# A top-k attention and two MLPs on one core: the products of p and v issued in one run, batch norms summed before their product

## The chip, the cores and the metric

The kernel runs on one core of a Trainium2 chip. The metric is the device time of one execution in microseconds (us): the median of the runs shown. All engines of the core work from queues of their own, each in the order in which its instructions were put there: PE (TensorE, matrix products; its weight loads are listed apart as PEld), DVE (VectorE), ACT (ScalarE), POOL (GpSimd) and SP (SyncE, which here issues DMAs).

## What is computed

The inputs q, k and v have the shape 4 x 8 x 576 x 64 (batch, heads, rows, columns), and the weights of each MLP are 512 x 2048 and 2048 x 512. The weights arrive as 64-bit floats, which the kernel converts itself.

```python
scores = scale * np.matmul(q, k.transpose(0, 1, 3, 2))
kth = np.partition(scores, -top_k, axis=-1)[..., -top_k:-top_k + 1]   # top_k = 32
scores = np.where(scores >= kth, scores, -1000000000.0)
scores = scores - np.max(scores, axis=-1, keepdims=True)
attn = np.exp(scores)
attn = attn / (np.sum(attn, axis=-1, keepdims=True) + 1e-09)
x = np.matmul(attn, v)                    # then to (B * S, H * D) = 2304 x 512
h = x @ w_in;  g = np.maximum(h, 0.0) + np.log1p(np.exp(-np.abs(h)));  x = g @ w_out
h = x @ w_in2; g = h - np.tanh(h);                                     out = g @ w_out2
```

## The kernel before

**Numbers.** Each operand of a product is split into a high and a low half of 16 bits, scaled by a power of two, and each product is the sum of three: high by high, high by low, low by high. The power of two comes from a sum of squares over the whole operand. `norm` (L332) takes it for one tensor of one batch: five pieces of 128 x 460 are loaded (L341), ACT squares each and leaves its row sums in one column of a tile `vss` of 128 x 5 (L343), and `col_norm` (L164) adds up partitions and columns on PE, by five products of one column with a matrix of ones (L169), accumulated in a tile `pn`. `pow2_scale` turns the sum into the scale and its inverse by three small DVE operations (L176, L179, L180). `v_norm` and `qk_norm` call it, for v and for q and k of a batch; the main loop does so at the tiles listed in `v_norm_at` and `qk_norm_at` (tiles 0, 4, 12 and 16, and for batches 2 and 3 tiles 40, 44, 56 and 60). Weight blocks, first visits and the MLP's middle activation go through `col_norm` too, with their own columns (`ss`, `qss`, `yss`).

**Attention.** It is cut into 144 tiles. 128 are normal: 128 rows of one head. Each head has 64 rows left over, and 16 further *left* tiles hold those of two heads. A tile goes through `front` (PE makes the scores `s`, L554; ACT copies them to `ssb`, L557), `chain` (DVE finds the 32 largest by four MAX8 and three MATCH_REPLACE8, L566 and L569), `exps` and `mask` (ACT, DVE L590), `turn` (ACT and POOL split p into halves `hl`, L596 to L598; SP issues a transposing DMA from `hl` to `pT`, L600) and `back`: PE multiplies `pT` by `vhl` into `px` (L612 to L617), ACT adds a small number to the sum column (L628), DVE takes its reciprocal (L629), ACT scales (L636). The product of a normal tile is 14 matmuls of 65 columns with weights of 128 x 128. That of a left tile is 28: 14 for each of two heads, with weights of 128 rows by 64 columns, which the profile shows as `128*64`.

**MLPs.** Their steps are fed in between, about one step of 256 rows for each attention tile: `gemm1` (24 products `h`, L680 to L682), `act1`, and some steps later `gemm2` (24 or 12 products `y`, L723 to L733). Weight conversion fills the first 420 us.

**Order.** The code is recorded in the order of the main loop; a scheduler then decides, engine by engine, in which order instructions are issued. It goes by a modelled timeline and by priorities: code under `tc.high_priority(n)` counts as if it stood n instructions earlier. `back` is called under `HP` = 50, as are `front` and `chain`; the first steps of the weight conversion have 100 and `act1` 100. On PE the order is fixed once made: an instruction that waits holds up all behind it.

Of the kernel before, what the change touches and what calls it, by code (L numbers as in the profile page):

```python
# [8 lines left out]
F32 = mybir.dt.float32  # L9
# [5 lines left out]
ALU = mybir.AluOpType  # L15
AX = mybir.AxisListType
# [51 lines left out]
LSP = 2  # L68
HID = 0
HP = 50  # L70


@with_exitstack
def topk_attention_two_mlps(
# [17 lines left out]
    nc = tc.nc  # L92
    P = 128
    B, H, S, D = q.shape
# [3 lines left out]
    NB = 4  # L98
# [46 lines left out]
    def tiny(n=1):  # L145
        o = used_[0]
        used_[0] += n
        return tiles_[:, o : o + n]
# [24 lines left out]
    def pow2_scale(ps, s, inv):  # L173

        n = sp.tile([P, 1], I32, tag="n0", name=nm("n0"))
        nc.vector.tensor_scalar(n, ps.bitcast(I32), 24, 23,  # L176
                                op0=ALU.logical_shift_right, op1=ALU.logical_shift_left)

        nc.vector.tensor_scalar(s.bitcast(I32), n, -1.0, float(204 << 23), op0=ALU.mult, op1=ALU.add)  # L179
        nc.vector.tensor_scalar(inv.bitcast(I32), n, float(50 << 23), None, op0=ALU.add)  # L180
# [150 lines left out]
    def norm(x, b, s, inv):  # L331
        xf = x[b].rearrange("h s d -> (h s d)").rearrange("(p n) -> p n", p=P)  # L332
        n = H * S * D // P
        np_ = -(-n // 512)
        w = n // np_ // 2 * 2
        ss = sp.tile([P, np_], F32, tag="vss", name=nm("vss"))
        for i in range(np_):
            o, e = i * w, (i + 1) * w if i < np_ - 1 else n
            j, st = xy_take([P, 512], F32, "vst")
            st = st[:, : e - o]  # L340
            nc.sync.dma_start(st, xf[:, o:e])  # L341
            xy_free.append(j)
            nc.scalar.activation(st, st, AF.Square, accum_out=ss[:, i : i + 1])  # L343
        pow2_scale(col_norm(ss, np_), s, inv)

    def v_norm(b):

        norm(v, b, sx[b], ix[b])

    def exp_scale(iq, ik, es, nes, nst):  # L350
        nc.vector.scalar_tensor_tensor(es, iq, QK, ik, op0=ALU.mult, op1=ALU.mult)
# [1 line left out]
        nc.vector.tensor_scalar(nst, es, -STEP, None, op0=ALU.mult)  # L353

    def qk_norm(b):
        norm(q, b, sq[b], iq[b])
        norm(k, b, sk[b], ik[b])
        exp_scale(iq[b], ik[b], es[b], nes[b], nst[b])

    def visit_norm(vi):  # L360

# [240 lines left out]
    def back(st):  # L602
        vi, it = st.vi, st.it
        ps = ps_t.tile([P, 512], F32, tag="tp", name=nm("px"))
        if st.kind == "n":
            sides = [(ps[:, 0 : D + 1], st.h, 0, P)]
        else:
            sides = [(ps[0:SL, j * (D + 1) : (j + 1) * (D + 1)], j, j * SL, (j + 1) * SL) for j in range(2)]
        for o, h, c0, c1 in sides:
            vh, vl = vi.vhl[:, 0, h], vi.vhl[:, 1, h]  # L610
            for t in range(NB):
                nc.tensor.matmul(o, st.pT[:, t, c0:c1], vh[:, t, 0 : D + 1], start=(t == 0), stop=False)  # L612
                nc.tensor.matmul(o, st.pT[:, t, c0:c1], vl[:, t, 0 : D + 1], start=False, stop=False)
                nc.tensor.matmul(o, st.pT[:, NB + 1 + t, c0:c1], vh[:, t, 0 : D + 1], start=False, stop=False)
            nc.tensor.matmul(o, st.pT[:, NB, c0:c1], vh[:, NB, 0 : D + 1], start=False, stop=False)

            nc.tensor.matmul(o, st.pT[:, NB, c0:c1], vl[:, NB, 0 : D + 1], start=False, stop=True)  # L617
        if st is it.sts[0]:
            it.x = ap.tile([P, 2, P], F16, tag="xs", bufs=NXS, name=nm("xs"))
            if XE:  # L620
                it.x32 = ap.tile([P, P], F32, tag="x32", bufs=NXS, name=nm("x32"))
        rows = P if st.kind == "n" else SL
        ns = len(sides)
        r = sp.tile([P, 2], F32, tag="r2", bufs=3, name=nm("r2"))

        pv = ps[0:rows, 0 : ns * (D + 1)].rearrange("p (j d) -> p j d", j=ns)
        rr = r[0:rows, 0:ns].unsqueeze(2)
        nc.scalar.activation(rr, pv[:, :, D : D + 1], AF.Identity, bias=(eps2 if st.soft else eps)[0:rows])  # L628
        nc.vector.reciprocal(r[0:rows, 0:ns], r[0:rows, 0:ns])  # L629
# [12 lines left out]
        if XE:  # L642
            if XE == 1:
                nc.scalar.copy(it.x[0:rows, 0, :], it.x32[0:rows])
            else:
                nc.vector.tensor_copy(it.x[0:rows, 0, :], it.x32[0:rows])
            nc.gpsimd.tensor_sub(it.x[0:rows, 1, :], it.x32[0:rows], it.x[0:rows, 0, :])
        nc.sync.dma_start_transpose(
            out=it.chunk.x.block(vi.p)[:, :, it.col : it.col + rows],
            in_=it.x[0:rows].rearrange("p r c -> p (r c)"),  # L650
        )
# [293 lines left out]
    c1 = [0]  # L945
# [55 lines left out]
        nonlocal_credit[0] -= st[0].T / 256.0  # L1001

    nonlocal_credit = [0.0]

    ensure_load(1)
    for i in range(LA - 1):
# [4 lines left out]
    for n in range(-1, NT + 2 + BL):  # L1011
        cur, prv, old, last = [tiles[i] if 0 <= i < NT else None for i in (n, n - 1, n - 2, n - 2 - BL)]
        if cur is not None:
          with tc.high_priority(HP):
            chain(cur)
            cur.ops[0]()
        if prv is not None:
          with tc.high_priority(HP):
            prv.ops[4]()
        if old is not None:  # L1020
            with tc.high_priority(HP):
                mask(old)
                turn(old)
        if last is not None:
            ch = last.it.chunk
            if not hasattr(ch, "x"):
                while ch.T // P > len(xy_free):
                    force_step(n - 2 - BL)
                ch.x = new_xy(ch.T, "x")
            with tc.high_priority(HP):  # L1030
                back(last)
        if n + 1 < NT and n + 1 >= 0:
            st = tiles[n + 1]
            st.vi = st.spec["vi"]
            with tc.high_priority(HP):
                front(st)
        if 0 <= n + LA < NT:
          with tc.high_priority(HP):
            prep_for(tiles[n + LA])
        if 0 <= n + 8 < NT:  # L1040
            ensure_load(tiles[n + 8].spec["i"] + 1)
        if n == VN:
            v_norm(0)
        if cur is not None and n >= VN and not hasattr(cur.vi, "vdone"):
            with tc.high_priority(HP):
                visit_prep_v(cur.vi)
                cur.vi.vdone = True
        if n >= 0:
            emit_steps(n - 2 - BL, 1)
            if n in qk_norm_at:  # L1050
                qk_norm(qk_norm_at[n])
            if n in v_norm_at and n > 0:
                b = v_norm_at[n]
                v_norm(b)
                if b % 2:
                    nc.vector.tensor_tensor(sxl[b // 2], sx[b - 1], sx[b], op=ALU.min)
                    nc.vector.tensor_tensor(ixl[b // 2], ix[b - 1], ix[b], op=ALU.max)
                    for c in (b - 1, b):
                        nc.vector.tensor_mul(fl[c], sxl[b // 2], ix[c])
            wcred[0] += WPS if wi[0] < 16 else (WPS2 if n >= W2N else 0)  # L1060
            while wcred[0] >= 1:
                wcred[0] -= 1
                conv_step()
            load_more()
        for i in (1, 2, 3):
          with tc.high_priority(HP):
            if cur is not None:
                cur.ops[i]()
            if prv is not None and i < 3:
                prv.ops[4 + i]()  # L1070
        if prv is not None:
            with tc.high_priority(HP):
                exps(prv)
# [34 lines left out]
```

## Time and profile before

| | |
|---|---|
| median of 3 runs | 1321.21 us (1319.98 to 1322.13) |
| the profiled execution | 1321.81 us |
| its span, first to last instruction | 1320.0 us |
| PE busy | 1040.3 us, 79% |
| DVE busy | 1015.6 us, 77% |
| ACT busy | 959.3 us, 73% |
| POOL busy | 843.6 us, 64% |

Busy time counts an instruction from its start to its end; products on PE overlap, so the time from one start to the next says more of them than their duration. The granted clock is the share of 2.4 GHz that TensorE got: 1.00 is 2.4 GHz and 0.50 is 1.2 GHz; a value between is a mean over both. In the chain of work that ended last, PE holds 47% of the span, DVE 16%, DMA 10%, POOL and ACT 9% each.

### The profile page before, as it was taken

The numbers are of one execution on the slowest core, as the hardware profiler recorded it, in microseconds if no ns is written. First come the engines' busy times: TensorE is split into PE (matmuls) and PEld (weight loads), VectorE is DVE, ScalarE is ACT, GpSimd is POOL, SyncE is SP. The second block draws the span as 40 slices with busy tenths as digits, with TensorE's granted clock in tenths as the row PEclk, the third lists the DMA queues.
The fourth block names the chain that finished last, engine by engine and source line by source line (L and its number), as shares of the span: only waits on it lengthen the run. The fifth ranks groups of instructions, "written<-read, shape, count | busy, mean of one in ns | idle before, by whom it ended". The sixth has DMA issues, their size and how long they took to land.

```text
span 1320.0 us, 27592 instructions
## 1 busy us (share of the span) xinstructions
PE 1040.3 (79%) x9778; PEld 811.4 (61%) x9778; DVE 1015.6 (77%) x2171; ACT 959.3 (73%) x1924; POOL 843.6 (64%) x1194
## 2 busy tenths in 40 slices
PE   2230335793347999899898999998999899999998
PEld 1120224682336876667666897676767777986975
DVE  5996988999999798977789889967889899610020
ACT  7987997987877788775778777758767777643332
POOL 2689865896877576565577766747776467643332
PEclk9999995896558999988899999989999899999999
DMA  8955886456565756644556444544445344300000
GB/s 270 289 173 154 251 215 150 116 122 159 128 146 133 173 102 151 139 87 85 108 114 130 94 87 89 104 95 95 110 97 116 71 93 96 51 6 9 9 9 16
DMA packets 322522, 153.14 MB, mean 116 GB/s; under 512 B 270160, under 2 KB 302416, under 8 KB 322384
## 3 DMA queue, kind: packets, MB, share of 16 engines
q1 hardware_dynamic: 322384, 151.39, 49.5%
q8 instruction: 76, 1.25, 0.4%
q14 instruction: 62, 0.51, 0.1%
HBM read 73.04 MB, written 15.37 MB: 67 GB/s over the span
## 4 chain that ended last, share of the span: by engine, by line
PE 47%; DVE 16%; DMA 10%; POOL 9%; ACT 9%; issue 8%; SPq 1%; POOLq 0%; ACTq 0%; DVEq 0%
PE h L682 7%; PE h L680 7%; PE h L681 7%; DVE m L566 5%; DVE x L569 5%; PE y L731 4%; PE y L732 4%; PE y L733 4%; PE y L723 3%; PE y L724 3%; PE y L725 3%; PE s L554 3%; POOL wlo L316 2%; DMA pT<-hl 2%; DVE x L590 2%
## 5 line engine op out<-in xcount | busy, mean ns | idle before, releaser
L566 DVE MAX8 m<-x 128x8 f32<-128x576 f32 x432 | 319.2, 749 | 3.4
L702 POOL TENSOR_SCALAR r<-r,gs 128x512 f32<-128x512 f32 (+1 forms) x160 | 109.3, 684 | 172.3 <-ACT g L701 168.7
L597 POOL TENSOR_TENSOR hl<-x,hl 128x512 f16<-128x512 f32 x144 | 172.7, 1199 | 71.5 <-ACT hl L596 58.6
L569 DVE MATCH_REPLACE8 x<-m,x 128x576 f32<-128x576 f32 x288 | 213.1, 740 | 0.0
L554 PE MATMUL s<-kT,qT 128*128 128x288 f16 x512 | 116.8, 321 | 97.9 <-ACT ssb L557 71.8
L705 POOL TENSOR_TENSOR g<-r,g 128x512 f16<-128x512 f32 (+1 forms) x160 | 172.8, 1080 | 8.8
L680 PE MATMUL h<-y,whi 128*128 128x256 f16 (+1 forms) x640 | 164.5, 265 | 5.9 <-ACT y L751 5.2
L681 PE MATMUL h<-x,whi 128*128 128x256 f16 (+1 forms) x640 | 166.7, 268 | 0.0
L680 PE MATMUL h<-x,whi 128*128 128x256 f16 (+1 forms) x640 | 166.5, 268 | 0.2
L682 PE MATMUL h<-x,wlo 128*128 128x256 f16 (+1 forms) x640 | 166.5, 268 | 0.0
L723 PE MATMUL y<-g,whi 128*128 128x256 f16 (+1 forms) x640 | 163.8, 266 | 2.8 <-DVE mx L420 2.7
L724 PE MATMUL y<-g,whi 128*128 128x256 f16 (+1 forms) x640 | 164.0, 265 | 1.4 <-POOL g L705 1.4
L681 PE MATMUL h<-y,whi 128*128 128x256 f16 (+1 forms) x640 | 164.2, 265 | 0.0
L725 PE MATMUL y<-g,wlo 128*128 128x256 f16 (+1 forms) x640 | 164.1, 266 | 0.0
L682 PE MATMUL h<-y,wlo 128*128 128x256 f16 (+1 forms) x640 | 164.0, 265 | 0.0
L699 DVE SCALAR_TENSOR_TENSOR r<-h,hin,r 128x512 f32<-128x512 f32 (+1 forms) x80 | 55.1, 690 | 141.1 <-ACT r L134 140.3
L134 ACT ACTIVATE r<-h,hin 128x512 f32<-128x512 f32 (+1 forms) x160 | 102.2, 640 | 82.7 <-PE h L682 69.4
L612 PE MATMUL px<-vhl,pT 128*128 128x65 f16 (+1 forms) x640 | 98.0, 208 | 67.9 <-DMA pT<-hl 55.1
L701 ACT ACTIVATE g<-r,gs 128x512 f16<-128x512 f32 (+1 forms) x160 | 107.8, 676 | 54.4 <-PE y L724 21.1
L566 DVE MAX8 m<-ssb 128x8 f32<-128x576 f32 x144 | 107.9, 750 | 42.5 <-ACT ssb L557 42.0
L680 PEld LDWEIGHTS <-whi 128*128 128x128 f16 x1280 | 127.5, 100 | 19.7
L681 PEld LDWEIGHTS <-whi 128*128 128x128 f16 x1280 | 127.1, 99 | 19.8 <-issue 1.8
(140 smaller groups left out, 3178.7 us busy)
## 6 DMA issues: line engine op xcount, KB each, us to landing
whi<-in_moe_w_in_dram SPq DMA_DIRECT2D x8, 1024.0 KB, 5.7
wlo<-in_moe_w_in_dram SPq DMA_DIRECT2D x6, 1024.0 KB, 7.2
wlo<-in_moe_w_out_dram SPq DMA_DIRECT2D x6, 1024.0 KB, 5.2
vd<-vhl SPq DMA_DIRECT2D x16, 330.0 KB, 2.9
vhl<-vd SPq DMA_DIRECT2D x16, 330.0 KB, 3.2
kd<-kT SPq DMA_DIRECT2D x32, 160.0 KB, 2.2
whi<-in_moe_w_out_dram SPq DMA_DIRECT2D x5, 1024.0 KB, 5.0
kT<-kd SPq DMA_DIRECT2D x32, 160.0 KB, 2.6
```

The lines of the kernel that those rows point to most:

```text
L554: nc.tensor.matmul(ps[:, hf, 0:HS], lhs, rhs[:, hf * HS : (hf + 1) * HS], start=(i == 0), stop=(i == len(prods) - 1))
L566: return lambda: nc.vector.max(m[:, 8 * i : 8 * i + 8], src)
L569: return lambda: nc.vector.match_replace(x, m[:, 8 * i : 8 * i + 8], src, NEG)
L597: nc.gpsimd.tensor_sub(hl[:, S + SL : 2 * S], st.p[:, 0 : NB * P], hl[:, 0 : NB * P])
L680: nc.tensor.matmul(o, hi[:, f], xhi, start=(d == 0), stop=False)
L681: nc.tensor.matmul(o, hi[:, f], xlo, start=False, stop=False)
L682: nc.tensor.matmul(o, lo[:, f], xhi, start=False, stop=(d == ND - 1))
L702: nc.gpsimd.tensor_scalar(r, r, gs, 1.0, op0=ALU.mult, op1=ALU.mult)
L705: nc.gpsimd.tensor_sub(glo, r, ghi)
L723: nc.tensor.matmul(o, hi[:, dd], gh, start=first, stop=False)
L724: nc.tensor.matmul(o, hi[:, dd], gl, start=False, stop=False)
L725: nc.tensor.matmul(o, lo[:, dd], gh, start=False, stop=fin)
```

## The change

`back` issues its products under a priority of 1000 instead of 50. `norm` returns a function that ends it: the five columns of `vss` are first summed on DVE to one column, which then goes through a single product in `col_norm`. For norms met at tile 20 or later that end is recorded two tiles after the squares. `vss` has two buffers by name.

```diff
+HPB = 1000
@@ norm
-        pow2_scale(col_norm(ss, np_), s, inv)
+        def finish():
+            tot = tiny()
+            nc.vector.tensor_reduce(tot, ss, axis=AX.X, op=ALU.add)
+            pow2_scale(col_norm(tot, 1), s, inv)
+        return finish
@@ back
-        for o, h, c0, c1 in sides:
-            ...
+        with tc.high_priority(HPB):
+            for o, h, c0, c1 in sides:
+                ...
@@ main loop
             if n in qk_norm_at:
-                qk_norm(qk_norm_at[n])
+                ends_at.setdefault(n if n < 20 else n + 2, []).append(qk_norm(qk_norm_at[n]))
...
+            for e in ends_at.pop(n, ()):
+                e()
```

What the scheduler makes of it. On PE, at left tile 64 (counted from 0; `px_7022` is its product, `pT_6909` its weights, `h` and `y` products of an MLP). Before, from the middle of the tile:

```order
L725 MATMUL y_6866<-g_6550,wlo_92 128x256
L613 LDWEIGHTS pT_6909
L613 MATMUL px_7022<-vhl_6505,pT_6909 64x65
L682 LDWEIGHTS wlo_90
L682 MATMUL h_6946<-x_3737,wlo_90 128x256
L614 LDWEIGHTS pT_6909
L614 MATMUL px_7022<-vhl_6505,pT_6909 64x65
L680 LDWEIGHTS whi_89
```

The same product now (`px_6986`; lines are 11 further down):

```order
L691 MATMUL h_6910<-x_3719,whi_89 128x256
L623 LDWEIGHTS pT_6873
L623 MATMUL px_6986<-vhl_6452,pT_6873 64x65
L624 LDWEIGHTS pT_6873
L624 MATMUL px_6986<-vhl_6452,pT_6873 64x65
L625 LDWEIGHTS pT_6873
L625 MATMUL px_6986<-vhl_6452,pT_6873 64x65
L623 LDWEIGHTS pT_6873
```

The 28 products stood in 27 pieces with MLP products between them, and stand in one. Over the kernel the 448 products of left tiles stood in 118 pieces and stand in 16; the 1792 of normal tiles stood in 543 pieces and stand in 198. The 70 joints that stay open there are between two normal tiles that alternate.

On PE, at normal tile 49, what stands ahead of its product. Before (`px_5362`):

```order
L733 MATMUL y_5138<-whi_95,g_4986 128x512
L731 LDWEIGHTS g_4985
L731 MATMUL y_5137<-whi_95,g_4985 128x512
L612 LDWEIGHTS pT_5261
L612 MATMUL px_5362<-vhl_4952,pT_5261 128x65
```

Now (`px_5335`):

```order
L692 LDWEIGHTS whi_93
L692 MATMUL h_5271<-y_3983,whi_93 128x256
L693 LDWEIGHTS wlo_94
L693 MATMUL h_5271<-y_3983,wlo_94 128x256
L623 LDWEIGHTS pT_5234
L623 MATMUL px_5335<-vhl_4925,pT_5234 128x65
```

It has moved ahead of 31 `y` products of 512 columns that stood before it.

## Rows read from the trace of the kernel before

**Rows 1.** The page: busy share in tenths over 40 equal slices, granted clock.

```profile
PE   2230335793347999899898999998999899999998
DVE  5996988999999798977789889967889899610020
PEclk9999995896558999988899999989999899999999
```

**Rows 2.** Busy time by stretch: start:end, length, engines (instructions), PE clock, DMA.

```profile
core 0: us, PE busy (x) PEld busy (x) DVE busy (x) ACT busy (x) POOL busy (x), PEclk, DMA share, GB/s
0.00:420.00 420.00, 180.97 (x1490) 143.06 (x1491) 373.34 (x808) 355.52 (x718) 307.04 (x392) 0.83 0.68 179
556.00:1010.00 454.00, 431.54 (x4180) 330.22 (x4181) 381.74 (x794) 330.04 (x664) 300.24 (x464) 0.96 0.48 100
1160.00:1320.00 160.00, 155.37 (x1360) 117.94 (x1356) 19.09 (x36) 53.79 (x86) 56.63 (x73) 1.00 0.03 10
```

**Rows 3.** Timeline of PE, left tile 64: start, duration, both us; full clock.

```profile
599.04 0.28 PE L680 MATMUL h<-x,whi 128*128 128x256 f16 x1
599.25 0.22 PE L615 MATMUL px<-vhl,pT 128*64 128x65 f16 x1
599.40 0.28 PE L681 MATMUL h<-x,whi 128*128 128x256 f16 x1
599.61 0.22 PE L617 MATMUL px<-vhl,pT 128*64 128x65 f16 x1
```

**Rows 4.** Timeline of PE, normal tile 81, full clock.

```profile
727.60 0.27 PE L682 MATMUL h<-x,wlo 128*128 128x256 f16 x1
727.71 0.19 PE L614 MATMUL px<-vhl,pT 128*128 128x65 f16 x1
727.74 0.27 PE L680 MATMUL h<-x,whi 128*128 128x256 f16 x1
```

**Rows 5.** Timeline of PE, left tile 64 and after it, half clock.

```profile
603.35 0.39 PE L682 MATMUL h<-x,wlo 128*128 128x256 f16 x1
603.67 0.26 PE L612 MATMUL px<-vhl,pT 128*64 128x65 f16 x1
603.87 0.39 PE L680 MATMUL h<-x,whi 128*128 128x256 f16 x1
...
606.35 0.42 PE L723 MATMUL y<-g,whi 128*128 128x256 f16 x1
606.56 0.42 PE L724 MATMUL y<-g,whi 128*128 128x256 f16 x1
```

**Rows 6.** Busy time by stretch, around left tile 64; columns as in rows 2.

```profile
593.00:602.00 9.00, 9.00 (x60) 5.52 (x57) 8.75 (x19) 5.14 (x10) 5.43 (x9) 1.00 0.27 67
602.00:606.00 4.00, 4.00 (x18) 1.82 (x18) 0.06 (x1) 0.66 (x1) 0.00 (x0) 0.53 0.00 0
606.00:609.00 3.00, 3.00 (x16) 2.13 (x16) 2.62 (x6) 1.74 (x6) 0.61 (x2) 0.50 0.52 98
```

**Rows 7.** Timeline of PE, unbroken normal tile 77 and left tile 90, first and last.

```profile
703.69 0.20 PE L612 MATMUL px<-vhl,pT 128*128 128x65 f16 x1 [1.21 <-DMA pT<-hl]
...
704.10 0.19 PE L617 MATMUL px<-vhl,pT 128*128 128x65 f16 x1
...
794.28 0.22 PE L612 MATMUL px<-vhl,pT 128*64 128x65 f16 x1
...
795.16 0.19 PE L617 MATMUL px<-vhl,pT 128*64 128x65 f16 x1
795.28 0.28 PE L680 MATMUL h<-y,whi 128*128 128x256 f16 x1
```

**Rows 8.** Waits from 300 us on: us in total, times, longest.

```profile
PE px L612 <- DMA pT<-hl: 16.6, 11, 4.1
DVE r L629 <- ACT r L628: 29.1, 10, 8.7
PE pn L169 <- ACT vst L343: 6.3, 5, 1.9
```

**Rows 9.** Tiles pn (400 to 560 us) and pT, line L416: ns min/median/max.

```profile
L169 PE MATMUL pn<-vss,tiny x60: 164/250/270, 408.3 to 556.3; 128*128 128x1 f32 x60
L416 DVE TENSOR_REDUCE mx<-t x6: 140/146/149, 150.7 to 536.6; 128x1 f32<-128x8 f32 x6
L612 PEld LDWEIGHTS <-pT x640: 95/98/292, 62.1 to 1160.3; 128*128 128x128 f16 x128, 128*64 128x64 f16 x32
DMA to landing us min/median/max: 3.2/3.3/7.4
```

**Rows 10.** Timeline of SP and PE, normal tile 49.

```profile
483.81 1.24 SPq L600 DMA_TRANSPOSE pT<-hl  x1
...
488.96 0.38 PE L731 MATMUL y<-whi,g 128*128 128x512 f16 x1
489.17 0.19 PE L612 MATMUL px<-vhl,pT 128*128 128x65 f16 x1
```

More of the change, by code (lines that the diff above doesn't have):

```diff
@@ L335, in norm @@
         w = n // np_ // 2 * 2
-        ss = sp.tile([P, np_], F32, tag="vss", name=nm("vss"))
+        ss = sp.tile([P, np_], F32, tag="vss", bufs=2, name=nm("vss"))
         for i in range(np_):
@@ L343, in norm @@
             nc.scalar.activation(st, st, AF.Square, accum_out=ss[:, i : i + 1])
-        pow2_scale(col_norm(ss, np_), s, inv)
+        def finish():
[3 more added lines that the diff above has]
+        return finish
     def v_norm(b):
-        norm(v, b, sx[b], ix[b])
+        return norm(v, b, sx[b], ix[b])
     def exp_scale(iq, ik, es, nes, nst):
@@ L355, in qk_norm, with finish @@
     def qk_norm(b):
-        norm(q, b, sq[b], iq[b])
-        norm(k, b, sk[b], ik[b])
-        exp_scale(iq[b], ik[b], es[b], nes[b], nst[b])
+        ends = norm(q, b, sq[b], iq[b]), norm(k, b, sk[b], ik[b])
+        def finish():
+            for e in ends:
+                e()
+            exp_scale(iq[b], ik[b], es[b], nes[b], nst[b])
+        return finish
     def visit_norm(vi):
@@ L608, in back @@
             sides = [(ps[0:SL, j * (D + 1) : (j + 1) * (D + 1)], j, j * SL, (j + 1) * SL) for j in range(2)]
-        for o, h, c0, c1 in sides:
[L610 to L617, printed above, removed]
+        with tc.high_priority(HPB):
+            for o, h, c0, c1 in sides:
+                vh, vl = vi.vhl[:, 0, h], vi.vhl[:, 1, h]
+                for t in range(NB):
+                    nc.tensor.matmul(o, st.pT[:, t, c0:c1], vh[:, t, 0 : D + 1], start=(t == 0), stop=False)
+                    nc.tensor.matmul(o, st.pT[:, t, c0:c1], vl[:, t, 0 : D + 1], start=False, stop=False)
+                    nc.tensor.matmul(o, st.pT[:, NB + 1 + t, c0:c1], vh[:, t, 0 : D + 1], start=False, stop=False)
+                nc.tensor.matmul(o, st.pT[:, NB, c0:c1], vh[:, NB, 0 : D + 1], start=False, stop=False)
+                nc.tensor.matmul(o, st.pT[:, NB, c0:c1], vl[:, NB, 0 : D + 1], start=False, stop=True)
         if st is it.sts[0]:
@@ L1003, in topk_attention_two_mlps, with left_scales @@
     nonlocal_credit = [0.0]
+    ends_at = {}
+    def left_scales(b):
+        nc.vector.tensor_tensor(sxl[b // 2], sx[b - 1], sx[b], op=ALU.min)
+        nc.vector.tensor_tensor(ixl[b // 2], ix[b - 1], ix[b], op=ALU.max)
+        for c in (b - 1, b):
+            nc.vector.tensor_mul(fl[c], sxl[b // 2], ix[c])
     ensure_load(1)
@@ L1042, in topk_attention_two_mlps @@
         if n == VN:
-            v_norm(0)
+            v_norm(0)()
         if cur is not None and n >= VN and not hasattr(cur.vi, "vdone"):
@@ L1050, in topk_attention_two_mlps @@
             if n in qk_norm_at:
-                qk_norm(qk_norm_at[n])
+                ends_at.setdefault(n if n < 20 else n + 2, []).append(qk_norm(qk_norm_at[n]))
             if n in v_norm_at and n > 0:
                 b = v_norm_at[n]
-                v_norm(b)
+                ends_at.setdefault(n if n < 20 else n + 2, []).append(v_norm(b))
                 if b % 2:
[L1056 to L1059, printed above, removed]
+                    ends_at[n if n < 20 else n + 2].append(lambda b=b: left_scales(b))
+            for e in ends_at.pop(n, ()):
+                e()
             wcred[0] += WPS if wi[0] < 16 else (WPS2 if n >= W2N else 0)
```

## The prediction

> **What bounds the kernel now.** I read the slices first, then the stretches, then PE's timeline inside the stretch that PE bounds. In the slices [rows 1] DVE leads up to about 420 us and PE from there on; after 1160 us only PE has work. The stretches say it in numbers [rows 2]. Up to 420 us DVE is busy for 373 us, PE for 181. From 556 to 1010 us PE is busy for 431.5 of 454 us and DVE for 381.7: PE stands still for 22 us, every other engine for over 70. After 1160 us it is PE alone, with 155 of 160. So from 556 us on time taken off PE is time taken off the end, as long as the others keep up.
>
> Busy is not useful, though. In that stretch PE has places where it is busy all the time and gets little done. In left tile 64, 602 to 606 us, PE is busy for 4.00 of 4.00 us and issues 18 products, while DVE is busy for 0.06, ACT for 0.66 and POOL not at all [rows 6]: the whole core waits for PE. The timeline shows why [rows 3]. A product of 64 weight columns (`128*64`) alternates there with an MLP product of the full array, and from one MLP product to the next it takes 0.36 us (599.04 to 599.40). Where the product of a normal tile is woven in in the same way, full array both, it takes 0.14 us (727.60 to 727.74) [rows 4]. So weaving as such is free (an MLP product takes 0.11 of it and px 0.03), but each change between 64 columns and 128, there and back, costs 0.22 us more. At the half clock a round takes 0.52 us (603.35 to 603.87) [rows 5].
>
> **The change part by part.** *Left tiles in one run.* The order has 118 pieces of left-tile products before and 16 after, so 102 rounds go. In the trace of before all but one of the 102 lie between 557 and 1009 us, in seven tiles, 77 at the full clock and 25 at half of it. At the full clock: 77 x (0.36 - 0.14) = 16.9 us. At the half clock a woven full-array round would take 0.21 (606.35 to 606.56) [rows 5] and twice 0.03, some 0.27: 25 x (0.52 - 0.27) = 6.3 us if the clock falls there all the same, and 25 x (0.52 - 0.14) = 9.5 us if it doesn't. The 28 products that are left in a run take 0.88 us and one change at either end, as left tile 90 does already (794.28 to 795.16) [rows 7]. I take 26.4 us, with 23.2 as the lower end. All of it is on PE in the stretch that PE bounds.
>
> *The clock.* It is 1.00 from 593 to 602 us, 0.53 from 602 to 606 and still 0.50 from 606 to 609, when ordinary MLP products run again [rows 6]. It fell while PE, by its busy time, never paused, in the middle of the alternation; the same happens in tiles 59 and 100, and together the three leave 11 us of ordinary work at half speed, worth up to 5.5 us. If the alternation brings it down, that comes back. If something else does, nothing. I take 4, the nearer row being that two of the three falls come late in the longest alternations.
>
> The Trainium skill, on the page "TensorE: Matmul & The Clock Gate" (Part 1: The HAM clock gate), ties the half rate to an idle engine. Rows 6 show a fall without a pause, so by that rule read plainly this part would be 0 and the sum 4 us less.
>
> *Normal tiles in one run.* 1792 products in 543 pieces become 198. A piece costs nothing by rows 4, so I take 0. Within a tile the last product comes some 1.3 us sooner (1.7 us from first to last where a tile is woven in, 0.41 in tile 77 [rows 7]), and DVE's reciprocal, which waited for 29.1 us in ten places from 300 us on [rows 8], waits less; that is part of how the other engines get their share of the gain, not a gain of its own.
>
> *The batch norms.* Six norms lie between 400 and 560 us, with 60 instructions on PE (two for each product) of 250 ns [rows 9]. 48 of them go, 24 products, 6 to 12 us depending on how far the two of a product overlap, and the waits of PE for the squares, 6.3 us [rows 8], go with them since the end is asked for two tiles later. Much of that lies where weight conversion and DMA still set the pace: bounds 0 and 18, I take 5. The 12 sums on DVE cost about what the reduction of 128 x 8 at L416 does, 0.146 us [rows 9]: 12 x 0.146 = 1.8 us, half of it where DVE leads. I take 1 us as a loss. What is queued behind them on DVE is the chain of the tile at hand; the squares they need lie two tiles back, so they should not wait.
>
> *What the higher priority moves.* The products of p and v stand earlier on PE, and PE holds everything behind one that waits for its `pT`. Before, 11 of some 120 tiles from 300 us on waited, 16.6 us in all [rows 8]; the others found their tile landed. Most tiles keep their place to within 1 us of matmul time. Seven stand 3 to 7.5 us earlier (42, 45, 49, 54, 58, 88, 89). Tile 49 is an example: its transpose is issued at 483.81, lands some 3.3 us later at the soonest [rows 9], and the product starts at 489.17 behind `y` products of 0.21 us each [rows 10], 31 of which it now passes, 6.6 us. Adding up for the seven what they move beyond what their tile had been waiting in memory gives some 15 us, and 18 with crumbs elsewhere: bounds 0 and 18. I take 5, since a wait of PE there lets DVE and ACT catch up and PE's later waits shrink.
>
> *The first 420 us.* Nearly every engine's order is shuffled there by a few places. DVE's idle time, 420 - 373 = 47 us [rows 2], is a bound on any gain; no row prices a loss. I take 0, with 6 to either side as in a few per cent of that idle time and a few weight passes.
>
> *What the others can't follow.* PE stands idle for 5% of 556 to 1010 us; with 30 us less work and DVE at 382 of 424, I let that grow to 10% of what is freed: 3 us lost.
>
> Sum: 26.4 + 4 + 5 - 1 - 5 - 3 = 26.4 us. The profiled execution took 1321.81, so 1295.4; the median of the runs stands 0.6 lower: 1295.
>
> **The rivals.** *The gain is half swallowed.* DVE, ACT and the transposes take PE's place in the stretch. From 640 us on slices with DVE at nine tenths are common [rows 1], and a tile needs about 5.5 us of DVE against some 6 of PE. Against it: in the broken tiles the other engines stand still [rows 6], so they gain their time there too. If half of the 30 us is lost: 1307.
>
> *PE waits for `pT`, and it ends slower.* The place is the head of PE's queue, L612 from 420 to 1160 us. The seven tiles give 18 us; and if the 16.6 us of waits that are there double, since less work stands ahead of each product, that is 35 us against 35 gained before this term and the last (26.4 + 4 + 5). It decides from about 35 us of new waits; with the norms' 5 us not coming either, 1321.8 - 30 + 35 = 1327. For it: on this queue the products now go before work that was ready. Against it: 110 of 120 tiles had landed, most for 1 to 8 us.
>
> *A run of small products is bound by its weight loads.* A load for these products lasts 98 ns [rows 9]; woven in, it lies under the MLP product ahead, 0.11 us long. If in a run each product took its load's 98 ns instead of 30, the 345 closed joints of normal tiles would cost 345 x 0.07 = 24 us, and the sum would come to 1321.8 - 26.4 + 24 = 1319. Against it: tile 77 runs its 14 in 0.41 us already, 30 ns each [rows 7]. The loads overlap each other.
>
> The Trainium skill states a load's time by its columns ("TensorE: Matmul & The Clock Gate", LDWEIGHTS), an estimate of 107 ns for 128 columns. By that rule the run would be load-bound, as this rival has it, and the kernel would come out at about 1322. The page also has a faster load for full 16-bit weights (Weight-path perf modes), and rows 7 side with that.
>
> *The change does not do what it says.* The order shows that it does on PE; only the time could fail to follow, which is the first rival.
>
> **How the numbers follow.** Forecast, 14 to 39 us gained: 0.76. Half swallowed, 3 to 14 gained: 0.13. PE's waits, slower: 0.05. Load-bound runs: 0.02, of which half ends within 0.2%. The rest, a first stage gone wrong or a mixture that ends near 1321: 0.04. A change of 0.2%, 2.6 us, is about what a measurement of this kernel can tell. Faster by more: 0.89; within: 0.05; slower: 0.06. The range takes in, above, 23.2 from the rounds, nothing from the clock, 2 from the norms, waits of 10 and the losses of 1 and 3 (11 us gained, 1311) and, below, 26.4 from the rounds, 5.5 from the clock, 10 from the norms, 1 lost to the sums and no waits (41 us gained, 1281).
>
> **What would show it.** In the profile after, left tiles appear as one run of 28 in about 0.9 us, and no stretch like 602 to 606 us is left, with DVE, ACT and POOL at rest. The stretch from tile 59 to tile 120, 556 to 1008 us before, takes 25 to 30 us less, and the time after the last attention tile stays at about 160 us. The clock is 1.00 around tiles 59, 64 and 100. `pn` from `vss` is gone and 12 reductions are there. I am wrong if PE's waits for `pT` grow by more than 15 us, if DVE is at 95% of the stretch, or if the first 420 us get longer.

## The result, and the profile after

The changed kernel took 1303.78 us, the median of 4 runs (1299.76 to 1307.39), against 1320.60 us for the kernel before beside it (1312.04 to 1322.13). The ratio is 0.9881, with a 95% interval from 0.9853 to 0.9910: 16.8 us gained, where 26 were forecast. The time lies inside the predicted range. The profiled execution of the changed kernel took 1306.19 us, 15.6 less than that of before.

The first view is the page of the kernel after, its slices, to be laid beside [rows 1].

```profile
PE   1221324884436999899799899998999899999998
DVE  5897889999999998899698879988989799510020
PEclk9999999896557999999799989998999899999999
```

DVE still leads up to about 420 us and PE behind it. From there to the last attention tile DVE is now mostly at eight or nine tenths, and the clock's slow places in the PE stretch stand elsewhere than before. The second view is the busy time by stretch, with the stretches of [rows 2] (the last ends with the span): start:end, length, each engine's busy time with its instructions, granted clock, DMA share, GB/s.

```profile
0.00:420.00 420.00, 172.40 (x1450) 133.94 (x1451) 370.29 (x812) 354.50 (x716) 308.00 (x393) 0.87 0.70 179
556.00:1010.00 454.00, 425.15 (x4329) 339.32 (x4328) 400.70 (x827) 344.34 (x690) 311.90 (x480) 0.97 0.50 104
1160.00:1304.00 144.00, 139.40 (x1137) 102.76 (x1134) 17.07 (x33) 47.33 (x75) 51.22 (x66) 1.00 0.03 10
```

By busy time the first 420 us are what they were. In the middle stretch PE gets through 149 more products in the same 454 us (4329 against 4180), and DVE is busy for 400.7 us instead of 381.7. So work was freed on PE and the others followed; but PE's own idle time has grown, from 22 to 29 us. The third view is PE's timeline at left tile 64 (start, duration, both in us), which answers to [rows 3].

```profile
588.05 0.27 PE L691 MATMUL h<-x,whi 128*128 128x256 f16 x1
588.25 0.22 PE L623 MATMUL px<-vhl,pT 128*64 128x65 f16 x1
...
589.13 0.19 PE L628 MATMUL px<-vhl,pT 128*64 128x65 f16 x1
589.34 0.27 PE L734 MATMUL y<-g,whi 128*128 128x256 f16 x1
```

The 28 products now take 0.88 us from the first to the last, with one change of columns at either end; before, they were strewn over some 12 us (593.9 to 605.8). The fourth view gives the waits from 300 us on (us in total, times, longest), beside [rows 8].

```profile
PE s L564 <- ACT ssb L567: 41.0, 21, 4.7
PE pn L170 <- ACT wlo L289: 30.1, 7, 10.0
DVE r L640 <- ACT r L639: 26.0, 16, 8.7
PE px L623 <- DMA pT<-hl: 10.0, 12, 2.0
```

The kernel before has for the first of these:

```profile
PE s L554 <- ACT ssb L557: 41.6, 17, 9.1
```

PE's waits for `pT` did not grow with the higher priority; they fell from 16.6 to 10.0 us, and the longest from 4.1 to 2.0. The waits for the copy of the scores are the same in sum, 41.0 and 41.6 us, but lie elsewhere, as is shown below. Those for `wlo`, 30.1 us, all lie ahead of 404 us, where DVE leads.

**Where the time came from.** A fixed amount of PE work can be compared in the two traces. I took PE's products in their order, without those of norms, each with its columns (at least 64) at 2.4 GHz, and looked at the part from 208 to 590 us of such work: 551.7 to 1013.6 us in the kernel before, 551.8 to 995.4 in the kernel after. The work is 382.2 us in both; it is an equal amount of work, not product for product the same, since the orders differ. What lies above it was put down to the reason at each product: a half clock, a change between 64 and 128 weight columns, PE idle ahead of the next product (wait), a norm's product, other.

| us | before | after | difference |
|---|---|---|---|
| length of the part | 461.9 | 443.6 | -18.3 |
| changes of columns | 27.9 | 3.5 | -24.4 |
| waits | 24.6 | 29.3 | +4.7 |
| half clock | 12.1 | 11.9 | -0.2 |
| products of norms | 4.0 | 4.6 | +0.6 |
| other | 11.1 | 12.2 | +1.1 |

Ahead of that part the kernel after is 0.1 us behind, and behind it it loses 2.3 us. Together that is 15.9 us gained; the profiled executions differ by 15.6.

**The new waits.** The waits of PE from 556 to 1010 us, the kernel before and then the kernel after:

```profile
PE px L612 <- DMA pT<-hl: 8.1, 6, 2.1
PE s L554 <- ACT ssb L557: 4.8, 4, 2.2
```

```profile
PE s L564 <- ACT ssb L567: 14.1, 10, 4.4
PE px L623 <- DMA pT<-hl: 5.3, 6, 2.0
```

What is late now is the copy of the scores: PE may write the next scores only when ACT has copied older ones, and it waits there for 14.1 us instead of 4.8. The longest such wait shows the clock as well. Busy time by stretch around it, and PE's line at its end:

```profile
735.00:745.00 10.00, 9.93 (x114) 8.99 (x113) 6.15 (x13) 7.53 (x16) 6.02 (x9) 1.00 0.33 67
745.00:750.00 5.00, 0.67 (x6) 0.52 (x6) 2.75 (x4) 3.45 (x7) 3.69 (x7) 0.99 0.00 0
750.00:757.00 7.00, 6.40 (x62) 5.78 (x61) 6.79 (x18) 4.63 (x13) 4.09 (x10) 0.52 0.40 84
```

```profile
749.33 1.08 PE L564 MATMUL s<-kT,qlT 128*128 128x288 f16 x6 [4.40 <-ACT ssb L567]
```

PE runs through ten busy microseconds, stands for 4.4, and has half the clock for the 7 that follow. A little earlier ACT and then DVE had been held up, which the same timeline shows on their engines:

```profile
735.89 0.62 ACT L513 CAST qhl<-qraw 128x512 f16<-128x512 f32 x1 [4.31 <-DMA qT<-qhl]
```

```profile
738.82 0.17 DVE L640 RECIPROCAL r<-r 128x1 f32<-128x1 f32 x1 [2.79 <-ACT r L639]
```

ACT waited 4.3 us for a buffer whose transpose was still under way, DVE then 2.8 us for ACT. That these led to PE's wait 10 us later is a reading of the order of events; no run tested it.

### The profile page after: what moved, and what is told of

Same layout as the page of the kernel before. It is cut to its first block, busy times and chain, and to the rows that moved or that the text cites. A ratio compares the mean times of both kernels' runs of the same rounds, so it can differ in the third digit from the quotient of the medians.

```text
span 1304.4 us, 27426 instructions
## 1 busy us (share of the span) xinstructions
PE 1007.8 (77%) x9682; PEld 793.1 (61%) x9682; DVE 1020.7 (78%) x2183; ACT 959.4 (74%) x1924; POOL 844.0 (65%) x1194
## 4 chain that ended last, share of the span: by engine, by line
PE 29%; DVE 22%; ACT 13%; DMA 13%; POOL 12%; issue 8%; SPq 2%; POOLq 0%; ACTq 0%; DVEq 0%
DVE m L576 7%; DVE x L579 7%; PE h L692 4%; PE h L691 4%; PE h L693 4%; DMA pT<-hl 2%; POOL hl L607 2%; PE y L735 2%; DMA qT<-qhl 2%; PE y L736 2%; PE y L734 2%; PE y L742 2%; PE y L743 2%; PE y L744 2%; POOL wlo L317 2%
## 5 line engine op out<-in xcount | busy, mean ns | idle before, releaser
L713 POOL TENSOR_SCALAR r<-r,gs 128x512 f32<-128x512 f32 (+1 forms) x160 | 112.5, 704 | 160.9 <-ACT g L712 158.8
L564 PE MATMUL s<-kT,qT 128*128 128x288 f16 x512 | 120.2, 326 | 98.2 <-ACT ssb L567 69.9
L734 PE MATMUL y<-g,whi 128*128 128x256 f16 (+1 forms) x640 | 163.1, 266 | 10.5 <-DVE y L763 6.9
L692 PEld LDWEIGHTS <-whi 128*128 128x128 f16 x1280 | 128.3, 100 | 23.4 <-issue 7.6
L693 PEld LDWEIGHTS <-wlo 128*128 128x128 f16 x1280 | 128.6, 101 | 13.7
L135 ACT ACTIVATE x<-ssb,nb,tiny 128x576 f32<-128x576 f32 x144 | 123.7, 865 | 15.3 <-DVE m L576 10.8
```

Source lines behind the costliest of these rows:

```text
L135: table[1].append(nc.scalar.activation(out, in_, func, **kw))
L564: nc.tensor.matmul(ps[:, hf, 0:HS], lhs, rhs[:, hf * HS : (hf + 1) * HS], start=(i == 0), stop=(i == len(prods) - 1))
L692: nc.tensor.matmul(o, hi[:, f], xlo, start=False, stop=False)
L693: nc.tensor.matmul(o, lo[:, f], xhi, start=False, stop=(d == ND - 1))
L734: nc.tensor.matmul(o, hi[:, dd], gh, start=first, stop=False)
```

## The experiments

Thirteen kernels in all, the changed one and twelve others, each compared with the kernel before on the same chip. The expectations number their theories, and each says what its theories are. Two numbers stand for the two halves of the kernel in the profiled execution of each: when the first 170 us of PE work (as above) were done, and how long the part from 208 to 590 us of work took. "Priority" is the high priority of the products of p and v.

| kernel | priority for | norms | median us | ratio, 95% | 170 us done at | part | changes | waits | half clock |
|---|---|---|---|---|---|---|---|---|---|
| before | none | old | 1320.6 | | 507.7 | 461.9 | 27.9 | 24.6 | 12.1 |
| after | all | new | 1303.8 | 0.9881 (0.9853 to 0.9910) | 508.8 | 443.6 | 3.5 | 29.3 | 11.9 |
| px_only | all | old | 1316.1 | 0.9987 (0.9966 to 1.0008) | 525.4 | 442.5 | 5.0 | 34.4 | 3.7 |
| norm_only | none | new | 1326.0 | 1.0065 (1.0036 to 1.0093) | 507.1 | 459.0 | 30.1 | 17.9 | 13.5 |
| full_before | none | old | 1313.6 | 0.9956 (0.9932 to 0.9980) | 510.2 | 444.7 | 0 | 37.1 | 9.2 |
| normal_only | normal tiles | old | 1336.1 | 1.0133 (1.0111 to 1.0155) | 519.6 | 468.6 | 28.3 | 23.4 | 16.0 |
| late_px | tiles from 48 | old | 1303.4 | 0.9861 (0.9837 to 0.9885) | 506.9 | 444.2 | 4.5 | 31.6 | 8.8 |
| late_left | left tiles from 48 | old | 1301.1 | 0.9845 (0.9816 to 0.9874) | 506.2 | 444.8 | 2.8 | 33.7 | 8.8 |
| late_after | tiles from 48 | new | 1299.9 | 0.9834 (0.9811 to 0.9858) | 512.3 | 442.3 | 2.9 | 31.4 | 9.3 |
| full_after | all | new | 1306.5 | 0.9879 (0.9851 to 0.9908) | 509.7 | 444.4 | 0 | 32.1 | 13.1 |
| early_px | tiles to 47 | old | 1344.9 | 1.0176 (1.0137 to 1.0215) | 523.2 | 472.9 | 28.1 | 27.2 | 19.8 |
| early_after | tiles to 47 | new | 1326.6 | 1.0054 (1.0024 to 1.0084) | 505.6 | 466.0 | 30.7 | 17.8 | 21.4 |
| nodelay | all | sum only | 1306.6 | 0.9888 (0.9846 to 0.9931) | 514.0 | 441.9 | 3.3 | 33.1 | 8.4 |
| delay5 | all | delay only | 1313.4 | 0.9943 (0.9920 to 0.9966) | 516.6 | 449.5 | 4.3 | 37.6 | 8.3 |

The kernel before took 1318.1 us (median) beside px_only to normal_only, 1320.7 beside late_px to full_after and 1320.5 beside the last four. One profiled execution stands beside each median, and runs of one kernel differ by some 5 us to either side, so single entries of the last five columns are read with that in mind, and the pattern rather than any one of them.

### The two halves apart: px_only and norm_only

The priority alone, with the norms as before:

```diff
+HPB = 1000
...
-        for o, h, c0, c1 in sides:
+        with tc.high_priority(HPB):
+            for o, h, c0, c1 in sides:
                 ...
```

> The kernel before with the first half of the change alone: the products of p and v under the priority of 1000, the norms as before. Left-tile products stand in 16 pieces, normal ones in 198, as with the whole change. If the gain is the joints of 64-column products (theory 1), this takes all of it: 1300 to 1308 us. If the sum of the norm's columns brings some 5 us of it (theory 3), it ends at 1306 to 1313.

And the norms alone, the priority left at 50 (of the norm's edit, two lines):

```diff
+            nc.vector.tensor_reduce(tot, ss, axis=AX.X, op=ALU.add)
+            pow2_scale(col_norm(tot, 1), s, inv)
```

> The second half alone: one product for a batch norm, two tiles late, and the products of p and v under the priority of before. The scheduler then lays the left-tile products in 174 pieces, 56 more than before. Theory 1: 56 rounds at 0.22 us are 12 us of PE, of which three quarters or so reach the end: 1325 to 1335, slower than before. Theory 3, the norm's own gain: 1313 to 1318.

px_only missed: with all the left tiles whole it gained nothing that can be told from 0. norm_only came out slower, as expected: by 0.4 to 0.9%. The reason expected for it, 56 more rounds, is not shown: most of them lie ahead of 545 us, the changes of columns in the part cost 30.1 us against 27.9, and the profiled execution, 1323.3 us, is only 1.5 longer than that of the kernel before. So neither half is faster by itself, and both together are, by 17 us; the parts don't add up. The table says where px_only lost it: its part from 208 us on is as short as that of the kernel after, but the first 170 us of work were done 17.7 us late. Most of the loss lies between 318 and 432 us. Busy time by stretch there, of px_only, and below of the kernel before and the kernel after:

```profile
318.00:432.00 114.00, 50.41 (x409) 38.39 (x406) 104.35 (x236) 84.38 (x207) 78.37 (x127) 0.57 0.55 124
```

```profile
318.00:432.00 114.00, 60.44 (x536) 48.41 (x534) 111.50 (x255) 89.89 (x223) 86.57 (x137) 0.65 0.59 137
```

```profile
318.00:432.00 114.00, 59.33 (x492) 46.90 (x493) 108.92 (x252) 91.76 (x228) 84.60 (x134) 0.60 0.61 143
```

DVE sets the pace here: 111.5 of 114 us in the kernel before. In px_only it is busy for 104.4 and has done 19 instructions fewer. The waits of PE in the same stretch, two lines of the kernel before and then those of px_only:

```profile
PE s L554 <- ACT ssb L557: 21.4, 7, 8.0
PE px L612 <- DMA pT<-hl: 7.7, 3, 4.1
```

```profile
PE s L555 <- ACT ssb L558: 36.1, 10, 7.2
PE px L614 <- DMA pT<-hl: 10.1, 3, 5.5
PE pn L170 <- ACT vst L344: 4.5, 1, 4.5
```

And one wait of DVE in px_only:

```profile
DVE m L567 <- ACT ssb L558: 4.5, 3, 2.4
```

PE's waits for the copy of the scores have grown by 14.7 us, those for `pT` by only 2.4, the longest from 4.1 to 5.5. DVE, which in the kernel before never waited for scores in this stretch, does so for 4.5 us. That a wait for `pT` at the head of PE's queue, with products of scores behind it, is what starts this is a reading of these lines; no run isolates it.

### Left tiles without a change of columns: full_before

The kernel before, but the products of a left tile use all 128 weight columns. The left rows of the second head of each left tile are left out by this. The number of products is the same; their order is not quite: products of left tiles stand in 123 pieces and those of normal tiles in 590 (118 and 543 before), and PE's order leaves that of the kernel before at 250 us.

```diff
-            sides = [(ps[0:SL, j * (D + 1) : (j + 1) * (D + 1)], j, j * SL, (j + 1) * SL) for j in range(2)]
+            sides = [(ps[:, j * (D + 1) : (j + 1) * (D + 1)], j, 0, P) for j in range(2)]
...
-            sc, src = r[0:rows, i : i + 1], o[:, 0:D]
+            sc, src = r[0:rows, i : i + 1], o[0:rows, 0:D]
```

> The kernel before, with the products of left tiles made on the full array: weights of 128 columns for each of the two heads, with the rows of both in the result and the first 64 kept (the second head's 64 left rows are so left out). Their products still stand between MLP products, in 123 pieces; normal ones in 590. Theory 1 (a change of weight columns is what costs): 20 us less PE, 1298 to 1308. Theory 2 (what costs is that the product is torn, whatever its columns): 1318 to 1326, as before.

The timeline of PE in left tile 64, still in pieces:

```profile
594.35 0.27 PE L682 MATMUL h<-x,wlo 128*128 128x256 f16 x1
594.46 0.19 PE L612 MATMUL px<-vhl,pT 128*128 128x65 f16 x1
594.49 0.27 PE L680 MATMUL h<-x,whi 128*128 128x256 f16 x1
594.60 0.19 PE L613 MATMUL px<-vhl,pT 128*128 128x65 f16 x1
```

And busy time by stretch there, the clock at 1.00:

```profile
585.00:595.60 10.60, 9.92 (x119) 8.73 (x118) 9.53 (x18) 9.12 (x17) 5.84 (x9) 1.00 0.71 125
```

A round takes 0.14 us (594.35 to 594.49), where it took 0.36 with 64 columns [rows 3]. It holds for all such rounds of one product of p and v between two MLP products of 256 columns at the full clock: 71 with 64 columns in the kernel before take 0.352 to 0.365 us, 356 in full_before 0.137 to 0.144. That shows the mechanism: the alternation of 64 and 128 columns costs 0.22 us a round, not the weaving. The median of 1313.6 us is 0.4% faster, some 5 us, which is less than expected, 1298 to 1308. The profiled execution took 1306.7 us, the least of ten runs that go up to 1318.5, and its part from 208 us on is 17 us shorter. So the price of a round is shown, but not how much of it reaches the median: late_left below, which loses nearly the same changes by whole products, gains 20 us. The other order of full_before may be the reason; no run separates the two.

### Normal tiles alone: normal_only

The priority for normal tiles; left tiles stay in 124 pieces.

```diff
+        with tc.high_priority(HPB if st.kind == "n" else 0):
```

> The priority of 1000 for normal tiles alone: their products stand in 198 pieces, as with the whole change, and those of left tiles in 124. Theory 1: no gain, 1315 to 1327. Theory 2 (whole products let DVE and ACT on sooner, whatever the columns): most of the gain, 1303 to 1310.

Slower than either theory had it, by 18 us against the kernel before. Early the priority loses 12 of the 18 us that px_only lost, and the late part is 6.7 us longer than before, 3.9 of them half clock. Whole normal products bring nothing there.

### Priority for the late tiles only: late_px, late_left, late_after

Here PE's early order is that of the kernel before (late_px and late_left, to 557 us) or of norm_only (late_after, to some 485 us). The edit, as late_after has it against the changed kernel:

```diff
-        with tc.high_priority(HPB):
+        with (tc.high_priority(HPB) if st.i >= 48 else ExitStack()):
```

> The kernel before, with the priority of 1000 for the products of tiles 48 to 143 alone; the norms as before. PE's order is that of the kernel before for its first 5005 rows, to about 555 us; from there left-tile products stand in one piece each. If the joints are the gain and what the priority does ahead of tile 48 took it away in the kernel with the priority alone (theory 1a), this has the gain without the loss: 1296 to 1304. If the gain of the stretch is swallowed later (theory 4), as before: 1312 to 1320.

In late_left the condition has `and st.kind == 'l'` as well.

> The same for the left tiles from 48 on alone (10 tiles): 101 rounds fewer, normal tiles torn as before (547 pieces). Theory 1a: the same time as with all tiles from 48 on, 1296 to 1305, within 3 us of it. Theory 2, whole normal products matter too: 5 us or more above it.

> The changed kernel with the priority of 1000 for tiles 48 to 143 alone: norms in one product, early tiles' products under the priority of before (left ones there in 18 pieces). If the norm's part matters only as what undoes the early loss of the priority (theory 1a), the time is that of the whole change within 5 us: 1298 to 1308. If norms and priority each give something on their own (theory 3): 1290 to 1297.

All three came out as expected, at 0.9861, 0.9845 and 0.9834 of the kernel before, with intervals that overlap. The old norms do as well as the new ones once the early tiles are left alone, so no gain of the norm change's own can be told from 0. And late_left, with 547 pieces of normal products against 196, does as well as late_px: the left tiles from 48 on are enough for the whole gain. Stretch 556 to 1010 us of late_left and PE's waits in it:

```profile
556.00:1010.00 454.00, 424.27 (x4361) 338.14 (x4360) 395.72 (x820) 340.39 (x688) 311.88 (x479) 0.98 0.51 104
```

```profile
PE px L614 <- DMA pT<-hl: 8.4, 11, 1.4
PE s L555 <- ACT ssb L558: 8.0, 9, 1.9
```

As in the kernel after, PE does more in the stretch and stands more. A priority for the left tiles from 48 on gives what the whole change gives. late_after's median is the lowest of all, 4 us below the changed kernel, with an interval (0.9811 to 0.9858) that touches that kernel's (0.9853 to 0.9910).

### The last changes of columns: full_after

The kernel after, left tiles on 128 columns by the same edit as in full_before; the left rows of the second head are left out again, and PE's order is that of the kernel after, product for product.

```diff
-            sides = [(ps[0:SL, j * (D + 1) : (j + 1) * (D + 1)], j, j * SL, (j + 1) * SL) for j in range(2)]
+            sides = [(ps[:, j * (D + 1) : (j + 1) * (D + 1)], j, 0, P) for j in range(2)]
```

> The changed kernel with the products of left tiles on the full array, in the order of the changed kernel on every engine, row for row (the second head's 64 left rows are left out). It takes away the 32 changes of weight columns that the changed kernel still has, some 0.1 us each. Theory 1: 3 us less PE, of which 1 to 3 reach the end: 1300 to 1304, or not to be told from the changed kernel's 1304.

0.9879 against 0.9881: no difference. With intervals of 4 us to either side, the 1 to 3 us expected of the last 32 changes can't be told from nothing.

### The early loss: early_px, early_after, nodelay, delay5

What in the new norms keeps the priority's early loss away? The first two kernels have the priority for the first 48 tiles only, with the old and the new norms:

```diff
+        with (tc.high_priority(HPB) if st.i < 48 else ExitStack()):
```

> The kernel before, with the high priority of the products of p and v for attention tiles below 48 alone; norms as before. Theory 1 (the priority alone loses time where DVE sets the pace: PE stands for pT at the head of its queue with scores behind it, and the late stage, left as it is, gives nothing back): slower, 1332 to 1340, the 13 to 18 us that px_only and normal_only had lost before 550 us. Theory 2 (px_only's early loss came from a profiled execution that was poor by chance, and the late tiles' priority decides): 1316 to 1324.

> The changed kernel, norms included, with the high priority for tiles below 48 alone; later tiles as in norm_only. Theory 1 (the changed norms keep the priority's early loss away, and the whole gain is in the left tiles from 48 on): 1318 to 1327, between the kernel before and norm_only, and some 12 us under early_px. Theory 2 (the early priority is worth something with these norms): 1308 to 1315. Theory 3 (the norms don't keep the loss away; something later in the changed kernel does): 1332 to 1345.

The other two have it for all tiles, and one half of the norm change each. nodelay keeps the sum and one product, but asks for the end where the squares are (shown for q and k; v likewise):

```diff
-                ends_at.setdefault(n if n < 20 else n + 2, []).append(qk_norm(qk_norm_at[n]))
+                ends_at.setdefault(n, []).append(qk_norm(qk_norm_at[n]))
```

> The changed kernel with every norm's end recorded where its squares are, not two tiles behind; the sum on DVE and the single product stay. Theory 1 (it is the two tiles of delay that keep the early loss away, since PE no longer stands for squares): 1312 to 1320, most of the early loss is back. Theory 2 (it is the sum, one product for five): 1300 to 1307. Theory 3 (neither; each shuffle of the early order deals the early waits anew): anything from 1300 to 1320, and not ordered with the next kernel by either part.

delay5 keeps the delay, with five products for each norm as before:

```diff
-            tot = tiny()
-            nc.vector.tensor_reduce(tot, ss, axis=AX.X, op=ALU.add)
-            pow2_scale(col_norm(tot, 1), s, inv)
+            pow2_scale(col_norm(ss, np_), s, inv)
```

> The changed kernel with five products for each norm, as before, but two tiles behind the squares; no sum on DVE. Theory 1 (the delay keeps the early loss away): 1300 to 1307, as the changed kernel. Theory 2 (the sum does): 1312 to 1320. Theory 3 (neither): anything from 1300 to 1320.

early_px is the slowest kernel of all, 24 us over the kernel before and above the 1332 to 1340 expected. Of the 24 us 15.5 are there when 170 us of work are done; its part from 208 us on is 11 us longer, 7.7 of them half clock. The priority isn't given there, but PE's order there is not quite that of the kernel before either (121 pieces of left tiles in all, not 118). early_after lies within the bounds expected of a kernel without the early loss: 505.6 us for the same work. So the new norms do keep it away.

By the halves, the work is done 17.7 us late with neither (px_only), 8.9 with the delay alone, 6.3 with the sum alone, 1.1 with both. A smaller amount of work tells the halves apart. 85 us of it were done at 403.5 us in the kernel before, ahead of the first norm that the change delays (408.3 us). The table has how much later than in the kernel before the eight kernels with the early priority got there, and what they lost from there to 170 us of work.

| kernel | norms | late at 85 us of work | lost from 85 to 170 |
|---|---|---|---|
| px_only | old | 11.9 | 5.8 |
| early_px | old | 9.8 | 5.7 |
| normal_only | old | 5.9 | 6.0 |
| delay5 | delay only | 9.7 | -0.8 |
| nodelay | sum only | 1.9 | 4.4 |
| after | new | 2.6 | -1.5 |
| full_after | new | 2.0 | 0.0 |
| early_after | new | 0.7 | -2.8 |

The kernels without the early priority were -0.4 to 3.7 us late at 85 us of work. So the loss has two steps: the sum keeps the first away, the delay the second. In the second step PE waits for a norm where the delay is missing: from 403 to 520 us for 8.2 us in px_only, 9.2 in early_px and 8.0 in normal_only, for the squares, and for 4.1 us in nodelay, for the sum on DVE; in delay5 for 1.7, and in the other three not at all. px_only's longest:

```profile
425.65 0.59 PE L170 MATMUL pn<-vss,tiny 128*128 128x1 f32 x2 [4.48 <-ACT vst L344]
```

That fits what the delay is for. But the kernel before waits there for 6.3 us as well [rows 8] and counts as on time, so the waits are not shown to be the whole cause. Why one product for five keeps the first step away stays open: the norms also shift what the scheduler puts where, and no run separates the two.

By the medians nodelay can't be told from the changed kernel (0.9888 and 0.9881), and delay5 lies between it and px_only (0.9943). Both times are those of theory 2, the sum, and of theory 3 as well, whose range takes in both. They don't rank the halves for the early loss: in the profiled executions most of what delay5 is behind nodelay lies in the late part (449.5 against 441.9 us).

## Why the prediction was right and wrong

**What bounds the kernel, and the rounds: right.** The 102 rounds were to give 26.4 us, 23.2 at the low end; the changes of columns fell by 24.4. full_before showed the price by itself, 0.36 against 0.14 us a round; it did not show that the median gets all of it. The 0.27 us that the prediction put together for a woven full-array round at the half clock are there in norm_only (12 rounds of 0.267 to 0.270). The Trainium skill says on the page "TensorEngine Tiling (Array Packing)" (Key Properties) that changing the tiling mode drains the engine. The trace agrees in that a product starts later behind a change, 0.21 and 0.15 us after the one ahead [rows 3] instead of 0.11 and 0.03 [rows 4]; no row shows the drain itself.

**The clock, 4 us: 0.2 in this kernel.** The falls at tiles 59, 64 and 100 are gone, as forecast, but others came (one of them behind the wait at 745 us), and the clock's share is 11.9 us against 12.1. The idea itself holds for tiles 64 and 100: there the clock fell, at 602.3 and 858.3 us, with no wait of PE in the 10 us ahead, and in full_before, where left tiles are torn as well but columns never change, no fall begins in a left tile. Tile 59 was misread: PE had waited for 1.26 us up to 555.10 and for 0.22 up to 556.89, and the clock fell at 557.9, after four changes of columns. The other two falls of the kernel before in the part, and all five of the kernel after, come within 3 us behind a wait of PE. Over all the kernels, the five with alternation lose 12.1 to 21.4 us to the half clock, the nine without 3.7 to 13.1. The step that failed was to count the gain as sure for one kernel: falls behind waits took the place of those in the alternation. Longer waits in sum don't mean more half clock, though (px_only 34.4 and 3.7 us, the changed kernel 29.3 and 11.9), so how much a kernel loses this way is not foreseen by any figure here.

**The norms, 5 us: 0.** The first 170 us of work were done at 508.8 us instead of 507.7. The products are gone, but PE does not set the pace there; the prediction had seen that ("weight conversion and DMA still set the pace") and counted 5 us all the same. late_px and late_after, with old and new norms, can't be told apart by time (0.9861 and 0.9834). What the norms are worth beside the early priority, 12 us of median (px_only 1316.1, the changed kernel 1303.8), comes from undoing its early loss, which the prediction did not have.

**Waits for `pT`, 5 us, and what the others can't follow, 3 us: 4.7 together**, and nearer the second by kind. The waits for `pT` fell; it is the scores' waits for ACT that grew in this stretch. The prediction also put DVE at 5.5 us a tile against some 6 of PE; the 381.7 us of [rows 2] over the 62 tiles from 59 to 120 are 6.2, so DVE stood closer behind PE than it reckoned. Over the nine kernels without alternation the waits are 29.3 to 37.6 us, against 17.8 to 27.2 in the five with it: some 11 us on the means (33.4 and 22.2), so about four tenths of the 26 that the changes of columns give (29.0 and 2.9); the clock gives 7.5 of it back on the means. The rival "half swallowed", 1307, was nearer to the median of 1303.8 than the forecast of 1295, and its mechanism, the other engines taking PE's place, is the one the waits show.

**The first 420 us, 0: right in sum, wrong in its parts.** A shuffle of a few places was priced at 6 us at most. The priority alone costs 16 to 18 us by the time 170 us of work are done (early_px, px_only), and the norms take it back. That the two cancel is luck, as far as the prediction goes: without its terms for the norms the same sum gives some 1299 us for the priority alone, and px_only took 1316.1. A term of 0 hid two large ones, and the price of "every engine's order is shuffled" had no row behind it.

**The sum.** From 208 to 590 us of work the prediction came to 26.4 + 4 - 5 - 3 = 22.4 us; it was 18.3. Ahead of it, 5 - 1 = 4 were forecast and 0.1 were lost. Behind it, 0 was forecast and 2.3 lost. That is 26.4 forecast and 15.9 measured: of the 10.5 missing, the norms and their sums are 4, the clock 4, the rounds 2, the tail 2, other small items 2, and the waits gave 3 back.

**The signs named beforehand.** The run of 28 in 0.9 us is there. `pn` from `vss` is gone, and 12 sums stand in its place on DVE, at 0.148 us as the row of L416 said [rows 9]:

```profile
L348 DVE TENSOR_REDUCE tiny<-vss x12: 138/148/158, 23.8 to 542.2; 128x1 f32<-128x5 f32 x12
```

PE's waits for `pT` did not grow by 15 us, DVE is at 88% of the stretch (400.7 of 454), and the first 420 us are hardly longer (2.6 us at 85 us of work). The sign that failed is the size: from the start of tile 59's product to the end of tile 120's it took 434.8 us instead of 451.4 (556.9 to 1008.3), 16.6 less and not 25 to 30. The time behind the start of the last attention product is 163.7 us instead of 159.3, since the last attention products moved ahead of 72 MLP products, 3.8 us of work. The load-bound rival fell: 28 products of 64 columns take 0.88 us in the run at tile 64, some 33 ns from one start to the next.

## What to carry to other kernels

Look in PE's timeline for products of different weight widths that alternate, and price a round against the same weaving at one width; that price holds, and here a priority for those few tiles was enough to collect it. Don't count on all of it where the next engine is close behind: three quarters arrived in this kernel's part (18.3 of 24.4 us), while PE's waits for that engine's copies grew, and in full_before only some 5 us of 27.9 reached the median. A priority that is meant for one stage should be given in that stage alone, since where another engine set the pace the same priority cost as much as was gained later.

## What was not expected of the hardware

Two edits of which neither is faster alone (px_only 0.9987, norm_only 1.0065) made 0.9881 together. Where several engines run close behind one another, as here, an edit's time can't be had by measuring it apart and adding.

A PE that is busy without a gap can lose its clock all the same: in left tile 64 it fell to the half with PE busy for 4.00 of 4.00 us [rows 6], in the middle of alternating weight widths, and in full_before, where the tile is torn as well but all widths are alike, the clock is 1.00 there.

Where PE was given a long uninterrupted run of work and then had to wait (745 to 749 us), the half clock that followed cost again: 7 us at 0.52 with PE busy for 6.40 of them are some 3 us of work lost, behind a wait of 4.4.
